# A fused attention and residual-MLP kernel on one core: scores three tiles per visit, second products tile by tile in two PSUM banks, first products with banks of their own

## The chip, the core and the metric

The kernel runs on one core of a Trainium2 chip. The metric is the device time of one execution in microseconds (us), lower is better. Engines are named as the profile names them: PE is TensorE (matmul), PEld its weight load, DVE is VectorE, ACT is ScalarE, POOL is GpSimd and SP is SyncE, whose queue here only starts DMAs.

## The reference

Two layers follow each other. The first is attention with 16 query heads on 4 key/value heads, the second a residual MLP with one product over tokens and two over channels:

```python
batch, n_q_heads, n_kv_heads, seq, head_dim = (8, 16, 4, 384, 64)
attn = softmax(q @ k.T / sqrt(64)); x = attn @ v      # per head; heads side by side give x: 8 x 384 x 1024
a1 = alpha1 * x + beta1
tok = np.einsum('ts,bsd->btd', w_tok, a1)             # 384 x 384
u = x + lam * tok
a2 = alpha2 * u + beta2
ch = np.maximum(a2 @ w_ch1, 0.0) @ w_ch2              # 1024 -> 4096 -> 1024
return u + lam * ch
```

## The kernel before, in words

**Stages.** Batches 0 and 1 are done one at a time (`main`, L526). Batches 2 to 7 are done as three pairs (`pair`, L661). A pair's two channel products are computed by the seven-product scheme that replaces the eight block products of a 2 x 2 block multiplication; the seven products are numbered 1 to 7 and called `o` in the code.

- *First products* (L693 to L738): 8 groups, each of 14 steps of 4 matmuls with 384 columns. Each step adds into one of the PSUM tiles X, Y or Z. ACT and DVE read these tiles, and the result `hid` stays in SBUF.
- *Second products* (L740 to L796): for each product `o` in the order 1, 2, 6, 5, 3, 7, 4, for each half `h` of the 16 contraction blocks `t`, for each of three token tiles `ms`, 8 matmuls with 512 columns into the PSUM tile C (L757). Three C tiles live through the whole stage. Products 2, 5, 3 and 4 add on top of what is already in PSUM, so that sums over products cost no engine. After the last half each C tile is read once (L778 to L785), by ACT for product 1 and by DVE for the others. DVE then scales the result (`scaled`, L675), and POOL adds it to the output by DMA (`store`, L519).

**The side work.** While PE does the second products of pair 0 and pair 1, the attention of the next two batches is slipped in between the C matmuls, as two "sides" (`side`, L230). Each side has 18 score tiles (`scores`, L272: 64-row matmuls, then one ACT exp over 128 x 1024), and for each of 8 head pairs `p`: `av` (L307: 18 small matmuls; then on DVE a reciprocal, a multiply into `xr`, and the two operations that make `a1`), `tok` (L341: 9 matmuls over tokens; then a DVE add and a multiply that makes `a2`), and `flip` (L420: SP spills `xr` to the output and transposes `a2` by DMA). For the last three head pairs of every second side `turn` (L429) does that transposition on PE, with a copy by ACT.

**What sets the order.** The order on each engine is the order in which the program is written (a manual schedule, L802). `pair` is a generator: in the second products it yields after every 4th matmul in effect, which makes 84 slots of 4 C matmuls. A dictionary `plan` says which side work is issued after which slot. For sides of batches 4 to 7 it is the table at L447 to L461: two score tiles every 4 slots (`scores2`), and `av`, `tok`, `flip` of head pair p at slots 4(p+1)+3, +6 and +8. The second of the two sides is shifted by 36 slots (L972). The operand sums for the next pair's first products (`sums_a`, L590, three DVE operations each) stand at slots 75, 75, 76 and 78 (L973), and `sum_w1` (L622) makes weight sums on DVE during product 4 (L746). The second-product weights (28 tiles of 512 KB, `w2s`) are fetched by SP (`fetch`, L636) into the ring `w1` of 6 slots; the last two tiles go to `pad`. The ring also takes the first-product weights (`load_w1`, L183, on POOL's queue).

**PSUM before.** The pairs have three pools that stay open to the end: `sc` (2 buffers of 2 banks: score tiles, `tok`, `turn`, and Y), `acc` (3 banks: X, C and one of the Z) and `one` (1 bank: `av`, and one of the Z).

Of the kernel before, what the change touches and what calls it, by code (L numbers as in the profile page):

```python
# [12 lines left out]
def kernel(  # L13
# [182 lines left out]
    def three():  # L196
        if pairs:
            return pairs["sc"].tile([P, 2, 4, P], f32, tag="sc", name="sc", bufs=2)
        return threes[0].tile([P, 2, 4, P], f32, tag="sc", name="sc", bufs=3)

    def one():
        if pairs:
            return pairs["one"].tile([P, 4, P], f32, tag="one", name="one", bufs=1)
        return three()[:, 0]
# [25 lines left out]
    def side(b):  # L230
# [72 lines left out]
        def scores2(i):  # L303
            for k in range(2):
                scores(2 * i + k)

        def av_piece(p, hh):  # L307
            if hh == 0:
                if first:
                    avs[p] = bank([P, 2, NST, D1], "mm", "av")  # L310
                else:
                    avs[p] = one().rearrange("p k s -> p (k s)")[:, :2 * NST * D1].rearrange(
                        "p (h st d) -> p h st d", h=2, st=NST)
            av = avs[p]
            hk = (2 * p + hh) // G
            for sq in range(NST):
                m = NST * hh + sq
                for sk in range(NST):
                    k = (p * NST + sk) * NST + m // 2
                    nc.tensor.matmul(out=av[:, hh, sq, :], lhsT=ess[k // 4][:, m % 2, k % 4, :],  # L320
                                     rhs=vb[:, sk, hk, :], start=(sk == 0), stop=(sk == NST - 1))
            if hh == 0:
                return
            rinv = sb.tile([P, 2, NST, 1], f32, tag="rinv", name="rinv", bufs=1)
            nc.vector.reciprocal(out=rinv, in_=av[:, :, :, D:])
            if not first:
                xr[p] = sb.tile([P, NST, P], f32, tag="xr", name="xr", bufs=3)
            nc.vector.tensor_tensor(out=x_of(p).rearrange("p st (h d) -> p h st d", h=2), in0=av[:, :, :, :D],  # L328
                                    in1=rinv.to_broadcast([P, 2, NST, D]), op=MUL)
            if first:  # L330
                return
            t = sb.tile([P, NST, P], f32, tag="a1f", name="a1f", bufs=2)
            nc.vector.tensor_tensor(out=t, in0=x_of(p), in1=bc(g1, p), op=MUL)
            a1s[p] = sb.tile([P, NST, P], bf, tag="a1", name="a1", bufs=2)
            nc.vector.tensor_tensor(out=a1s[p], in0=t, in1=bc(h1, p), op=ADD)  # L335
# [100 lines left out]
        if not first:  # L436
# [10 lines left out]
            if (b - NPL) // 2 > 0:  # L447
# [5 lines left out]
                for j in range(9):  # L453
                    put(4 * j, scores2, j)
                for p in range(NP):
                    put(4 * (p + 1) + 3, av, p)
                    put(4 * (p + 1) + 6, tok, p)
                    put(4 * (p + 1) + 8, flip, p)
                    if by_pe(p):
                        put(4 * (p + 1) + 8 + (p == NP - 3), turn, p)  # L460
# [175 lines left out]
    def fetch(i, n, at=None):  # L636
        if at is None:
            w2_slots[i, n] = w1_free.pop(0)
            at = ring[:, w2_slots[i, n]]
        else:  # L640
            w2_slots[i, n] = None
        w2_at[i, n] = at
        nc.sync.dma_start(out=at, in_=w2s[n])

    def free(slot):
        if slot is None:
            return
        w1_free.append(slot)
        if queue:
            f, *a = queue.pop(0)  # L650
            f(*a)

    queue = [m for i in range(NB) for m in [(load_w1, c) for c in order1[2 if i else RING:]]
             + [(fetch, i, n) for n in range(SLOTS - 2 if i + 1 < NB else SLOTS)] + [(load_w1, c) for c in order1[:2] if i + 1 < NB]]
# [5 lines left out]

    def pair(i):  # L661
        b0 = NPL + 2 * i
        acc = pairs["acc"]
# [3 lines left out]
        def begin_end(ms):  # L667
            ends[ms] = t = piece().bitcast(f32)
# [6 lines left out]
        def scaled(o, b, ms, dw, t):  # L675
            if o != 2:
# [11 lines left out]

        def finish(ts):
# [3 lines left out]
        for g in range(NH // 2):  # L693
            X, Y, snap = {}, {}, {}
            for k, (o, e) in enumerate(SEQ1):
                t = 2 * g + e
                lo, hi = bias1[:, t:t + 1], bias1[:, NH + t:NH + t + 1]
                if o == 1:
                    X[e] = acc.tile([P, 512], f32, tag="acc", name="X", bufs=3)
                if o == 7:  # L700
                    Y[e] = pairs["sc"].tile([P, 2, 512], f32, tag="sc", name="Y", bufs=2)[:, 0]
                if o == 2:
                    Z = acc.tile([P, 512], f32, tag="acc", name="Z", bufs=3) if e else pairs["one"].tile(
                        [P, 512], f32, tag="one", name="Z", bufs=1)
# [35 lines left out]
        X = [[(0, 512, acc.tile([P, 512], f32, tag="acc", name="C", bufs=3))] for _ in range(NST)]  # L740
        snap = {}
        where = {2: (0, 0), 3: (0, 1), 7: (1, 1), 4: (1, 0)}
        for k, o in enumerate(PLACE2):
            for h in range(2):
                for ms in range(NST):
                    if o == 4 and not last and 1 < 3 * h + ms < 5:  # L746
                        sum_w1(0, (5, 7, 6)[3 * h + ms - 2])
                    if o == 5 and not last and h and ms < 2:
                        fetch(i, SLOTS - 2 + ms, pad[:, (1 + ms) * 2048:(2 + ms) * 2048])
                    if last and (o, h) in ((6, 1), (7, 0)):  # L750
                        (lift_end if o == 7 else begin_end)(ms)
                    if last and (o, h, ms) == (7, 0, NST - 1):
                        X[ms] = [(c0, c1, pairs["sc"].tile([P, 2, 512], f32, tag="sc", name="C", bufs=2)[:, 0, :c1 - c0])
                                 for c0, c1 in ((0, 384), (384, 512))]
                    for (c0, c1, x), t in ((c, t) for c in X[ms] for t in range(8 * h, 8 * h + 8)):
# [3 lines left out]
                                         start=(o in (1, 6, 7) and t == 0), stop=(t == NH - 1), skip_group_check=True)  # L759
                        if t % 4 == 3 and ms == NST - 1 and c1 == 512:  # L760
# [6 lines left out]
                        if t % 8 == 3 and c1 == 512:  # L767
                            flush(1)
                            yield 1
                    if h == 1 and not (last and o == 4):  # L770
# [6 lines left out]
                        for c0, c1, x in X[ms]:  # L777
                            if o == 1:  # L778
                                nc.scalar.copy(out=snap[o, ms], in_=x)
                            elif o in (6, 5):  # L780
                                tt(out=snap[o, ms], in0=x, in1=snap[1, ms], op=ADD)
                            elif o == 2:
                                tt(out=t, in0=x, in1=lam_t[:, :512], op=MUL)
                            else:
                                tt(out=t[:, c0:c1], in0=x, in1=snap[{3: 1, 7: 5, 4: 6}[o], ms][:, c0:c1], op=ADD)  # L785
                        if o not in (1, 6, 5):
                            later.append((scaled, o, b0 + bb, ms, dw, t))
                    if o in (2, 6) and (h, ms) in ((0, 1), (0, 2), (1, 0), (1, 1)):
                        r = [(0, 1), (0, 2), (1, 0), (1, 1)].index((h, ms))
                        ts = slice(4 * r, 4 * r + 4)  # L790
                        if o == 2:
                            tt(out=hid[:, ts, 0], in0=hid[:, ts, 3], in1=hid[:, ts, 0], op=SUB)
                        else:
                            tt(out=hid[:, ts, 4], in0=hid[:, ts, 4], in1=hid[:, ts, 0], op=SUB)
# [5 lines left out]
    with tc.manual_schedule(engines=order):  # L800
# [162 lines left out]
        for i in range(NB - 1):  # L963
# [6 lines left out]
            for u, f, h in ((10, flip_q, 0), (17, flip_k, 0), (18, flip_q, 2), (25, flip_q, 4), (33, flip_k, 2), (33, flip_q, 6)):  # L970
                put(ps, 1, u, f, c + 1, h, 2)
            put_all(ps, 1, side(c + 1)[1], lambda u: u + 36)  # L972
            for j, u in ((1, 75), (0, 75), (2, 76), (3, 78)):  # L973
                put(ps, 1, u, sums_a, j)
        for ps in range(NPL + NB):
# [8 lines left out]
            if ps == NPL - 1:  # L984
                side_banks.close()
                mm_banks.close()
                for name in ("sc", "acc", "one"):
                    pairs[name] = ST(tc.psum_pool(name=name, bufs=3))
# [3 lines left out]
        assert not plan  # L992
# [28 lines left out]
```

## Time and profile before

| | |
|---|---|
| median of 3 runs | 743.85 us (743.79 to 745.54) |
| the profiled execution's own time | 745.27 us |
| its span, from the first to the last instruction | 743.5 us |
| granted TensorE clock, mean | 0.999 |
| DVE busy, share of the span | 69% |
| ACT busy, share of the span | 43% |
| main(0) and main(1) until PE starts the first products of pair 0 | 244.2 us |
| pair 0: first products, second products with two sides | 72.8 us, 101.9 us |
| pair 1: first products, second products with two sides | 73.0 us, 101.9 us |
| pair 2: first products, second products without sides | 72.9 us, 72.8 us |

The stage times are the starts of the first matmul of each stage on PE in the trace. In a timeline each row gives the start in us from the span's start, the length in us, the engine, the line, the operation with out<-in, and how many instructions the row merges; a bracket at the end gives the idle time of the engine before the row and what ended it. A row of a windows table gives a stretch, its length, and then for PE, PEld, DVE, ACT and POOL the busy time with the number of instructions, the granted clock, the DMA share and GB/s.

### The profile page before, as it was taken

Reading aid. Unit: us, or ns where it says so; the run is one execution under the profiler, and the core shown is the slowest. Engines: PE = TensorE matmul, PEld = TensorE weight load, DVE = VectorE, ACT = ScalarE, POOL = GpSimd, SP = SyncE. Lnnn points to the kernel's source line nnn. Section 1 sums busy time; section 2 is a strip of 40 time slices with the busy share of each in tenths; the row PEclk is TensorE's granted clock in tenths of the full one; section 3 lists DMA queues with packets and bytes.
Section 4 is the critical chain, followed back from the end, with each engine's and each line's share of the span. In section 5 each row is a group of like instructions: output and inputs, shape, how many; then the busy total and the mean of one; then the engine's idle time right before and its main releaser. Section 6 shows DMA issues by size and latency. Waiting matters only on the chain.

```text
span 743.5 us, 14441 instructions
## 1 busy us (share of the span) xinstructions
PE 731.1 (98%) x5708; PEld 416.1 (56%) x5769; DVE 514.6 (69%) x998; ACT 319.3 (43%) x458; POOL 163.4 (22%) x211
## 2 busy tenths in 40 slices
PE   8999999999999999999999999999999999999997
PEld 5866555566555566645555566655555566654444
DVE  7763366567687889748778977747957987762354
ACT  7632431334332566653443366664334166660000
POOL 9434220420000232201003433210002331000011
PEclk9999999999999999999999999999999999999999
DMA  9999999999998999999979999998988998935976
GB/s 185 194 201 200 207 219 168 172 184 204 221 275 243 178 222 214 256 219 213 272 246 205 200 174 174 173 216 181 246 278 221 183 165 115 162 117 176 291 210 158
DMA packets 218017, 151.32 MB, mean 204 GB/s; under 512 B 88660, under 2 KB 197060, under 8 KB 217948
## 3 DMA queue, kind: packets, MB, share of 16 engines
q0 software_dynamic: 120304, 64.60, 65.8%
q1 hardware_dynamic: 97100, 85.39, 42.3%
q8 instruction: 45, 0.74, 0.4%
q10 hardware_dynamic: 544, 0.39, 0.2%
q14 instruction: 24, 0.20, 0.1%
HBM read 154.84 MB, written 38.27 MB: 260 GB/s over the span
## 4 chain that ended last, share of the span: by engine, by line
PE 85%; DMA 8%; POOL 2%; issue 2%; DVE 2%; POOLq 0%; DVEq 0%
PE C L757 29%; PE X L707 17%; PE Y L707 8%; PE ch L575 8%; PE h L537 7%; PE Z L707 4%; PE sc L280 4%; PE sc L345 3%; DMA ops<-a 3%; DMA w<-in_moe_w_ch_dram 2%; PE one L320 2%; DMA q_raw<-in_q_dram 2%; PE sc L320 1%; POOL w L185 1%; DMA rows<-in_moe_lam_dram 1%
## 5 line engine op out<-in xcount | busy, mean ns | idle before, releaser
L757 PE MATMUL C<-w,arena 128*128 128x512 bf16 (+2 forms) x949 | 219.9, 372 | 2.3
L289 ACT ACTIVATE es<-sc 128x1024 bf16<-128x1024 f32 x126 | 121.8, 1022 | 162.7 <-PE sc L280 158.6
L757 PEld LDWEIGHTS <-arena 128*128 128x128 bf16 x1040 | 93.7, 98 | 99.8 <-issue 7.6
L712 ACT ACTIVATE hT<-X,bias 128x384 f32<-128x384 f32 x144 | 83.7, 581 | 67.4 <-PE X L707 60.4
L707 PEld LDWEIGHTS <-w 128*128 128x128 bf16 x768 | 75.1, 98 | 50.3 <-issue 0.4
L185 POOL DMA_DIRECT2D w<-in_moe_w_ch_dram x68 | 62.4, 924 | 128.9 <-PE X L707 68.2
L575 PE MATMUL ch<-arena,hT 128*128 128x512 bf16 x366 | 87.9, 379 | 1.0 <-issue 0.3
L522 POOL DMA_DIRECT2D out_dram<-hT x33 | 29.3, 887 | 261.5 <-DVE hT L677 135.7
L537 PE MATMUL h<-ops,w 128*128 128x384 bf16 (+1 forms) x480 | 83.7, 327 | 1.9 <-DVE hT L548 0.9
L707 PEld LDWEIGHTS <-pad 128*128 128x128 bf16 x576 | 56.4, 98 | 37.2
L707 PE MATMUL X<-ops,w 128*128 128x384 bf16 x384 | 70.5, 326 | 0.0
L707 PE MATMUL X<-ops,pad 128*128 128x384 bf16 x384 | 70.3, 326 | 0.0
L537 PEld LDWEIGHTS <-w 128*128 128x128 bf16 x480 | 45.1, 98 | 32.3 <-issue 2.8
L575 PEld LDWEIGHTS <-hT 128*128 128x128 bf16 x384 | 34.7, 98 | 36.8 <-issue 2.5
L352 DVE TENSOR_TENSOR xr<-sc,xr 128x384 f32<-128x384 f32 x56 | 31.1, 555 | 34.1 <-PE sc L345 34.1
L320 PEld LDWEIGHTS <-es 128*128 128x128 bf16 x1008 | 38.3, 97 | 12.4
L280 PE MATMUL sc<-qT,kT 64*128 64x384 bf16 (+2 forms) x576 | 43.8, 272 | 0.9 <-DVE xr L328 0.2
L345 PEld LDWEIGHTS <-wtokT 128*128 128x128 bf16 x576 | 37.4, 98 | 12.9 <-DVE a L335 2.7
L707 PE MATMUL Z<-ops,w 128*128 128x384 bf16 x192 | 39.1, 326 | 0.0
L707 PE MATMUL Y<-ops,w 128*128 128x384 bf16 x192 | 39.1, 326 | 0.0
L714 DVE TENSOR_TENSOR arena<-Y,hT 128x384 bf16<-128x384 f32 x48 | 26.8, 558 | 17.3 <-ACT hT L712 15.0
L345 PE MATMUL sc<-a,wtokT 128*128 128x128 bf16 x504 | 37.3, 219 | 0.1
(140 smaller groups left out, 858.2 us busy)
## 6 DMA issues: line engine op xcount, KB each, us to landing
w<-w2s SPq DMA_DIRECT2D x80, 512.0 KB, 4.7
w<-in_moe_w_ch_dram POOLq DMA_DIRECT2D x68, 512.0 KB, 9.9
out_dram<-xr SPq DMA_DIRECT2D x56, 192.0 KB, 5.6
out_dram<-hT POOLq DMA_DIRECT2D x33, 256.0 KB, 6.9
arena<-in_moe_w_ch_dram POOLq DMA_DIRECT2D x16, 512.0 KB, 19.8
w2s<-arena SPq DMA_DIRECT2D x28, 256.0 KB, 3.5
q_raw<-in_q_dram POOLq DMA_DIRECT2D x28, 192.0 KB, 10.4
w2s<-pad SPq DMA_DIRECT2D x16, 256.0 KB, 2.7
```

Of the source, the lines that this page charges most:

```text
L185: nc.gpsimd.dma_start(out=w1[:, w1_slots[c]], in_=w1src[:, :, c * CW * P:(c + 1) * CW * P])
L280: nc.tensor.matmul(out=sc[:, hh, k % 4:k % 4 + n], lhsT=kT[r, 2 * p // G, BLK[hh][sk], :], rhs=qT[r, p, st:st + n, :], start=True, stop=True)
L289: nc.scalar.activation(out=e, in_=sc, func=EXP, scale=scale_qk)
L320: nc.tensor.matmul(out=av[:, hh, sq, :], lhsT=ess[k // 4][:, m % 2, k % 4, :], rhs=vb[:, sk, hk, :], start=(sk == 0), stop=(sk == NST - 1))
L345: nc.tensor.matmul(out=ps[:, tt, :], lhsT=wtokT[:, st, tt * P:(tt + 1) * P], rhs=a1s[p][:, st, :], start=(st == 0), stop=(st == NST - 1 an ...
L352: nc.vector.tensor_tensor(out=u, in0=ps, in1=u, op=ADD)
L522: nc.gpsimd.dma_start(out=at, in_=o, accum_op=ADD)
L537: nc.tensor.matmul(out=ps[:, :n], lhsT=w1[:, w1_slots[c], dt, j * P:(j + 1) * P], rhs=a2T[:, dt, :n], start=(dt == 0), stop=(dt == NDT - 1))
L575: nc.tensor.matmul(out=ps, lhsT=hT[:, nt, ms * P:(ms + 1) * P], rhs=w2[:, row(nt)[0], row(nt)[1], cs], start=(i == 0), stop=(i == NNT - 1))
L707: nc.tensor.matmul(out=ps, lhsT=tb[g, o][:, dt, e * P:(e + 1) * P], rhs=opb(LEFT1[o])[:, dt], start=(o in (1, 2, 7) and dt == 0), stop=(dt ...
L712: nc.scalar.activation(out=snap[o, e], in_=ps, func=IDENT, bias=hi if o == 5 else lo)
L757: nc.tensor.matmul(out=x, lhsT=hid[:, t, LEFT2[o], ms * P:(ms + 1) * P], rhs=rhs[:, t % 4 * 512 + c0:t % 4 * 512 + c1], start=(o in (1, 6, ...
```

## The change

- **Score visits.** The table for the sides of batches 4 to 7 has six visits of three score tiles (`scores3`) at slots 0, 6, 12, 21, 26 and 31 in place of nine visits of two. In two of the six visits the third exp is issued after the next `av`. `av`, `tok` and `flip` (now directly behind `tok`) get new slots. The second side is shifted by 39 slots, and `sums_a` moves to slots 78, 78, 80 and 82.
- **Second products tile by tile.** In pairs 0 and 1, for all products but 4, one C tile takes all 16 contraction blocks at once. It starts from zero in one of two banks, so the sums over products that PSUM made before are now made by DVE: product 2 is added to product 1 and scaled later, product 7 is read twice.
- **Banks.** The pools are no longer open to the end. `share_banks` closes the pools of one stage and opens those of the next: X (3 banks), Y (3) and Z (2) for the first products; `sc` (3 buffers of 2 banks, now also for `av`) and `acc` (2 banks) for the second products.
- **Buffers and fetches.** `xr` has four buffers instead of three and `a1f` one instead of two. Two places in `pad` join the ring for the second-product weights, so that eight tiles can be there. Four first-product weight chunks of the next pair are loaded early instead of two. In pair 2, the tiles `ends` lie in the `es` buffers.

The core of the diff:

```diff
     def three():
         if pairs:
-            return pairs["sc"].tile([P, 2, 4, P], f32, tag="sc", name="sc", bufs=2)
+            return pairs["sc"].tile([P, 2, 4, P], f32, tag="sc", name="sc", bufs=3)
...
     def one():
-        if pairs:
-            return pairs["one"].tile([P, 4, P], f32, tag="one", name="one", bufs=1)
         return three()[:, 0]
...
-                xr[p] = sb.tile([P, NST, P], f32, tag="xr", name="xr", bufs=3)
+                xr[p] = sb.tile([P, NST, P], f32, tag="xr", name="xr", bufs=4)
...
-            t = sb.tile([P, NST, P], f32, tag="a1f", name="a1f", bufs=2)
+            t = sb.tile([P, NST, P], f32, tag="a1f", name="a1f", bufs=1)
...
-                for j in range(9):
-                    put(4 * j, scores2, j)
+                for j in range(6):
+                    put((0, 6, 12, 21, 26, 31)[j], scores3, j, j in (2, 5))
                 for p in range(NP):
-                    put(4 * (p + 1) + 3, av, p)
-                    put(4 * (p + 1) + 6, tok, p)
-                    put(4 * (p + 1) + 8, flip, p)
+                    put((4, 10, 14, 18, 24, 29, 33, 35)[p], av, p)
+                    put((8, 15, 17, 22, 27, 34, 36, 38)[p], tok_flip, p)
                     if by_pe(p):
-                        put(4 * (p + 1) + 8 + (p == NP - 3), turn, p)
+                        put((37, 39, 41)[p - NP + 3], turn, p)
...
+    def padded(i, n):
+        return n % 8 > 5 or i + 1 < NB and n >= SLOTS - 2
+
+    def fetch(i, n):
+        w2_slots[i, n] = slot = (pad_free if padded(i, n) else w1_free).pop(0)
+        w2_at[i, n] = ring[:, slot] if slot < RING else pad[:, (slot - RING + 1) * 2048:(slot - RING + 2) * 2048]
+        nc.sync.dma_start(out=w2_at[i, n], in_=w2s[n])
...
+    for i in range(NB):
+        heads = [(load_w1, c) for c in order1[:4]] if i + 1 < NB else []
+        queue += [(load_w1, c) for c in order1[4 if i else RING:]] + [(fetch, i, n) for n in range(SLOTS - 2)] + heads[:2]
+        queue += [(fetch, i, n) for n in (SLOTS - 2, SLOTS - 1)] + heads[2:]
...
+    pair_banks = ExitStack()
+
+    def share_banks(*names):
+        pair_banks.close()
+        for name in names:
+            pairs[name] = pair_banks.enter_context(tc.psum_pool(name=name, bufs=3))
+
     def pair(i):
         b0 = NPL + 2 * i
-        acc = pairs["acc"]
+        share_banks("X", "Y", "Z")
...
         def begin_end(ms):
-            ends[ms] = t = piece().bitcast(f32)
+            ends[ms] = t = sb.tile([P, 512], f32, tag="es", name="ends", bufs=EB)
...
         def scaled(o, b, ms, dw, t):
-            if o != 2:
+            if o != 2 or not last:
...
         finish(slice(NH - 2, NH))
-        X = [[(0, 512, acc.tile([P, 512], f32, tag="acc", name="C", bufs=3))] for _ in range(NST)]
+        share_banks("sc", "acc")
...
         for k, o in enumerate(PLACE2):
-            for h in range(2):
+            whole = not last and o != 4
+            for h in range(1 if whole else 2):
                 for ms in range(NST):
...
+                    if whole:
+                        X[ms] = [(0, 512, acc.tile([P, 512], f32, tag="acc", name="C", bufs=2))]
+                    elif not last and h == 0:
+                        X[ms] = c_banks(ms)
+                    upto = NH if whole else 8 * h + 8
...
-                                tt(out=snap[o, ms], in0=x, in1=snap[1, ms], op=ADD)
-                            elif o == 2:
+                                tt(out=snap[o, ms], in0=x, in1=snap[1 if last or o == 6 else 6, ms], op=ADD)
+                            elif o == 2 and last:
                                 tt(out=t, in0=x, in1=lam_t[:, :512], op=MUL)
                             else:
-                                tt(out=t[:, c0:c1], in0=x, in1=snap[{3: 1, 7: 5, 4: 6}[o], ms][:, c0:c1], op=ADD)
+                                base = {2: 1, 3: 1 if last else 5, 7: 5, 4: 6}[o]
+                                tt(out=t[:, c0:c1], in0=x, in1=snap[base, ms][:, c0:c1], op=ADD)
+                            if o == 7 and not last:
+                                tt(out=snap[6, ms], in0=x, in1=snap[6, ms], op=ADD)
...
-            for u, f, h in ((10, flip_q, 0), (17, flip_k, 0), (18, flip_q, 2), (25, flip_q, 4), (33, flip_k, 2), (33, flip_q, 6)):
+            for u, f, h in ((10, flip_q, 0), (17, flip_k, 0), (18, flip_q, 2), (28, flip_q, 4), (33, flip_k, 2), (33, flip_q, 6)):
                 put(ps, 1, u, f, c + 1, h, 2)
-            put_all(ps, 1, side(c + 1)[1], lambda u: u + 36)
-            for j, u in ((1, 75), (0, 75), (2, 76), (3, 78)):
+            put_all(ps, 1, side(c + 1)[1], lambda u: u + 39)
+            for j, u in ((1, 78), (0, 78), (2, 80), (3, 82)):
                 put(ps, 1, u, sums_a, j)
```

The helper `c_banks(ms)` gives the C tile of product 4: from `acc` for the first two token tiles and from `sc` for the third. `pad_free`, `pump` and the new `free` let a fetch wait in the queue until a ring slot or a place in `pad`, whichever it needs, is free.

## The prediction

> **What bounds the kernel now.** I read the page first, then the stages, then the starts of PE's rows, then DVE where the stages meet. Part 1 of the page:
>
> ```profile
> PE 731.1 (98%) x5708; PEld 416.1 (56%) x5769; DVE 514.6 (69%) x998; ACT 319.3 (43%) x458; POOL 163.4 (22%) x211
> ```
>
> PE is busy for 98% of the span at a granted clock of 0.999. Only fewer PE microseconds can make the kernel faster, and any wait put on PE makes it slower by its full length. The windows table over the second products of pair 0 (with two sides) and of pair 2 (without):
>
> ```profile
> 317.00:418.90 101.90, 100.95 (x905) 53.62 (x921) 74.81 (x147) 38.23 (x43) 13.98 (x16) 1.00 1.03 229
> 666.70:739.50 72.80, 72.42 (x363) 34.66 (x367) 30.55 (x46) 2.11 (x4) 7.68 (x9) 1.00 0.75 218
> ```
>
> The sides cost PE 29.1 us per pair, and there DVE is busy for 74.8 of 101.9 us: PE never waits long for it, but it is not far from full. PE's timeline at the end of that stage:
>
> ```profile
> 402.27 1.02 PE L757 MATMUL C<-w,arena 128*128 128x512 bf16 x4
> 403.23 0.61 PE L280 MATMUL sc<-qT,kT 64*128 64x256 bf16 x8
> 403.77 1.04 PE L757 MATMUL C<-w,arena 128*128 128x512 bf16 x4
> ...
> 410.50 0.67 PE L345 MATMUL sc<-a,wtokT 128*128 128x128 bf16 x9
> ...
> 418.94 1.61 PE L707 MATMUL X<-ops,w 128*128 128x384 bf16 x8
> ```
>
> Elsewhere in the stage eight C matmuls take 1.73 us from start to start (327.28 to 329.01), so a slot of four takes 0.865. Here four take 0.96 because 64-row matmuls follow: 0.10 is lost on entering a score visit. The visit then takes 0.54 for two tiles whose columns, two row halves at a time, need 0.43: about 0.10 is lost on leaving. A visit costs **0.19** beside its tiles. `av` takes 0.53, `tok` 0.50, `turn` 0.17.
>
> DVE's timeline over the same end, from tok of the last head pair (L352) to the third C tile of product 4 (L785):
>
> ```profile
> 411.20 0.56 DVE L352 TENSOR_TENSOR xr<-sc,xr 128x384 f32<-128x384 f32 x1 [0.44 <-PE sc L345]
> 411.79 0.56 DVE L356 TENSOR_TENSOR obuf<-xr,vecs 128x384 bf16<-128x384 f32 x1
> 412.27 0.35 DVE L591 TENSOR_TENSOR ops<-ops 128x384 bf16<-128x384 bf16 x1
> ...
> 414.13 0.69 DVE L631 TENSOR_TENSOR pad<-w 128x1024 bf16<-128x1024 bf16 x1
> ...
> 417.19 0.69 DVE L785 TENSOR_TENSOR hT<-C,hT 128x512 f32<-128x512 f32 x1
> ...
> 418.99 0.69 DVE L785 TENSOR_TENSOR hT<-C,hT 128x512 f32<-128x512 f32 x1
> ...
> 420.32 0.68 DVE L785 TENSOR_TENSOR hT<-C,hT 128x512 f32<-128x512 f32 x1
> ```
>
> DVE works without a gap and reads the last C tile at 421.00, **2.1 us after PE has begun the next stage** at 418.94. Nothing waits for that today: of the first X tiles the second waits 0.15 for its own bank (the row at 418.94 is 1.61 long where others of x8 are 1.46).
>
> **The change, part by part.** The sum is made against the profiled execution: span 743.5, its own time 745.27, while the median of the runs is 743.85. I add the sum to the median.
>
> *Score visits.* Four sides with 6 visits instead of 9: 12 visits fewer, 12 x 0.19 = **-2.3 us**. The matmuls stay the same in number and shape, and the C matmuls are only reordered (216 ns each either way).
>
> *Small waits of before.* Per pair, in the starts of PE's rows: two `tok` 0.10 late, one `turn` 0.15, the X tile 0.15. All stand at places that the change rebuilds; I take them as gone, 2 x 0.5 = **-1.0** (bound: 0).
>
> *Banks: a wait at each stage change.* In the changed kernel's instruction order the first X matmul of a pair waits not for the reader of its own bank but for DVE's read of the last tile of the pools just closed: the third C tile of product 4 for pairs 1 and 2, the last ch tile of main(1) for pair 0. Behind this waiting instruction stands all of PE. The price for pair 0 can be read today:
>
> ```profile
> 244.23 1.46 PE L707 MATMUL X<-ops,w 128*128 128x384 bf16 x8
> 244.43 0.69 DVE L582 TENSOR_TENSOR obuf<-ch,vecs 128x512 f32<-128x512 f32 x1 [1.57 <-PE ch L575]
> ```
>
> DVE ends at 245.12; with 0.06 until PE starts (as after the 0.15 wait above), X starts **0.95** late. That is the bare price with an idle DVE, and the lower bound for the other two. There DVE is behind. I count from the end of slot 72. PE: av(6) 0.53, slot, tok(5) 0.50, slot, av(7) 0.53, slot, tok(6) 0.50, slot, turn 0.17, slot, 0.15 for its buffer, tok(7) 0.50, five slots of 0.865 in all: tok(7) ends at 7.2. Then six slots and two turns, 5.5: the stage ends at 12.7. DVE, in the new order: two reads and a scaling of product 7's last tile until 1.3; av(6) 1.88 (reciprocal 0.19 and three of 0.56; 402.72 to 404.60 today); tok(5) 1.06; av(7) 1.88; tok(6) 1.06; one weight sum 0.60: tok(7)'s add starts at 7.75. From there to the end of the last C read is today 421.00 - 411.20 = 9.80, with three weight sums; the new order has the same operations but one weight sum (0.60) ahead of tok(7): 9.20. The last read ends at 16.95, and PE starts X at 17.0 instead of 12.7: **4.3 us**, twice: +8.6. The lag grew from 2.1 because tok(7) moves from slot 74 to 77 and av(7) from 71 to 74, while 9 us of DVE work stay behind it. After the wait DVE is less behind than today, so nothing else is late in the first products; `sum_w1` and the X, Y, Z reads there have 56.5 of 73.0 us.
>
> *Closer side work.* DVE must make `a1` between av and tok, and read av before the third score tile may take its buffer. First side, counted from the end of slot 33: av(6) is made by 2.6, a `hid` difference 0.88, tok(5) 1.06, a C read 0.60, av(7) 1.88: `a1` of pair 7 is there at 7.1. PE wants tok(7) at 6.4 (five slots 4.33, two av 1.06, two tok 1.0): +0.8 with waking. Counting slots 12 to 26 alike, x of av(4) ends at 17.4 when the third tile of the fifth visit wants it: 0.1 to 0.2 late with the weight load. The second side has no `hid` differences and pays only the 0.15 above, which the 12.7 holds and the 4.3 does not. Two pairs: 2 x (0.8 + 0.2) = **+2.0** and 2 x 0.15 = **+0.3**. The bounds are 0 and, with both places on each side, 4.
>
> *At nothing.* The DVE additions (product 7 read twice, product 2 scaled: 6 x 0.69 per pair) lie in DVE's idle 27 us, and where not they are in the ledgers. ACT's three exps (3 x 1.02) end before the av that wants them, 2 to 4 slots later. `a1f` is written and read by DVE alone. `xr` has four buffers for spills that land in 5.6 us. The SP flips wait for DVE directly behind `tok`, with fetches behind them; a weight tile is wanted 10 or more slots after its fetch and lands in 4.7. The last two go to `pad` at slots 70 and 71 and are wanted at slot 78: 7 slots and seven visits, 9.6 us, against 6.3 for the pad row. The later flip_q is wanted 23 slots on. The end of pair 2 keeps its order.
>
> Sum: -2.3 - 1.0 + 0.95 + 8.6 + 2.0 + 0.3 = **+8.55**: 743.85 + 8.55 = **752.4 us**.
>
> [...]
>
> **Rivals.**
> 1. *The wait does not bind (faster or even).* Place: first X of each pair. If DVE's last read were done when PE arrives, or PE did not wait for it, the result is -3.3 to -1.0: 740.6 to 742.9. It decides from a DVE lag of 0. Against: even an idle DVE needs 0.95 after the last matmul. Chance 0.03.
> 2. *DVE keeps up.* Three boundaries at 0.95, clusters 0 to 2.3: -3.3 + 2.85 + 0 to 2.3: 743.4 to 745.7. It needs DVE to lose 3.3 us of work before the boundary; the rows show it gapless over the last 9.8. Chance 0.05.
> 3. *Also a late transfer.* The two pad tiles (3.3 us of margin), with two weight loads of 9.9 us issued at the same slots. If they land 2 us late in both pairs: 756.4. For it: the DMA share is 1.3 in 402 to 419. Against: the ring has more room than before. Chance 0.10.
>
> The forecast (749 to 755.5) has 0.82. The range leaves out rivals 1 and 2 and the far part of 3: 747.5 to 756. A measurement of this kernel tells about 0.3% (2.2 us): faster 0.03, within it 0.05, slower 0.92.
>
> **What would show it.** Right: an idle stretch of about 4 us on PE before the first X of pairs 1 and 2, ended by DVE's read of a C tile, and 0.95 before pair 0; 24 visits of 64-row matmuls in place of 36; first products still 73 us; second products with sides 1 us shorter before waits. Wrong: X starting directly after C, or PE waits on DMA in the last slots.

## The result, and the profile after

The changed kernel takes 754.28 us (median of 5 runs, 752.46 to 756.75), the kernel before 744.49 us beside it (743.79 to 745.54): a ratio of 1.0129, interval 1.0104 to 1.0155. It is slower by 1.3%; the forecast was 752.4 us. The profiled run is the fastest of the five: 752.46 us, with a span of 750.7 us at a mean clock of 0.997. The engines' line of its page, and then the windows of the first products of pair 0, its second products, the first and second products of pair 1, and the second products of pair 2 (columns: length, then busy time and count of PE, PEld, DVE, ACT and POOL, granted clock, DMA share, GB/s):

```profile
PE 729.8 (97%) x5710; PEld 419.1 (56%) x5769; DVE 521.3 (69%) x1010; ACT 318.7 (42%) x458; POOL 163.4 (22%) x211
```

```profile
243.28:316.09 72.81, 72.81 (x449) 43.85 (x450) 62.43 (x116) 48.49 (x80) 22.36 (x28) 1.00 1.25 210
316.09:421.45 105.36, 99.64 (x905) 54.55 (x921) 80.23 (x157) 38.10 (x43) 15.94 (x19) 1.00 1.01 224
421.45:495.93 74.48, 74.48 (x449) 44.42 (x449) 54.01 (x99) 48.49 (x80) 23.18 (x29) 0.98 1.25 179
495.93:601.30 105.37, 99.80 (x906) 54.57 (x921) 80.25 (x157) 38.10 (x43) 15.01 (x17) 1.00 0.97 215
674.10:747.00 72.90, 72.39 (x362) 34.65 (x367) 30.63 (x46) 2.08 (x4) 7.66 (x9) 1.00 0.75 218
```

PE's busy time in the second products with sides fell from 100.95 to 99.6 to 99.8 us, as fewer visits should make it, and yet each of these stages grew from 101.90 to 105.4 us. So 5.6 to 5.7 us of each is waiting, where it was 0.95. Pair 0's first products and pair 2's second products are as they were. Pair 1's first products are 1.5 us longer, with PE busy throughout but a clock of 0.98. What ended PE's waits, over the whole span (total, times, longest):

```profile
PE X L720 <- DVE hT L818: 5.3, 2, 3.1
PE C L781 <- DMA pad<-w2s: 2.6, 3, 1.8
...
PE sc L339 <- DVE a L329: 1.2, 2, 0.6
PE X L720 <- DVE obuf L575: 0.8, 1, 0.8
```

L818 is DVE's read of a C tile (L785 before), L339 is `tok`, L575 the read of the lead's last ch tile. PE's timeline at the end of pair 0, then DVE's over the same end:

```profile
414.53 1.89 PE L781 MATMUL C<-pad,arena 128*128 128x512 bf16 x8 [1.76 <-DMA pad<-w2s]
...
421.45 1.83 PE L720 MATMUL X<-ops,w 128*128 128x384 bf16 x8 [2.28 <-DVE hT L818]
423.08 1.49 PE L720 MATMUL Y<-ops,w 128*128 128x384 bf16 x4
...
426.38 0.81 PE L720 MATMUL Y<-ops,w 128*128 128x384 bf16 x4
```

```profile
412.12 0.55 DVE L346 TENSOR_TENSOR xr<-sc,xr 128x384 f32<-128x384 f32 x1
...
415.64 0.68 DVE L818 TENSOR_TENSOR hT<-C,hT 128x512 f32<-128x512 f32 x1
...
418.37 0.68 DVE L818 TENSOR_TENSOR hT<-C,hT 128x512 f32<-128x512 f32 x1
...
420.62 0.68 DVE L818 TENSOR_TENSOR hT<-C,hT 128x512 f32<-128x512 f32 x1
```

DVE starts the add of the last `tok` at 412.12 and ends the last C read at 421.30; X starts at 421.45, where the kernel before had let X start 2.1 us ahead of the end of that read. The bracket at 414.53 is a wait the sum did not have: the second of the two pad tiles of product 4 is late (the four matmuls on the first one started at 411.58 without a wait). From the starts of PE's rows the two waits are 1.92 and 2.44 us here, 4.36 together; in pair 1 they are 1.14 and 3.22 us, again 4.36. The row at 423.08 shows a third thing: four matmuls take 1.49 us where four take 0.81 later, half speed: the granted clock is 0.50 from 423.0 to 424.5.

The profiled spans differ by 7.2 us: +3.5 in each of two second products, +1.5 in pair 1's first products, +0.9 in front of pair 0, -0.3 behind the last products, and -1.9 in the lead stages, 1.4 of it in main(1)'s first products (57.7 before, 56.3 after). The attention that runs there uses the buffers of `xr` and `a1f`, whose number the diff changes. In the kernel before, PE waits there for transfers (0.60 us at 133.55 for `ops`, 0.26 us at 152.47 for a weight load); in the changed kernel and in every variant below these two waits are gone. That is 0.86 of the 1.4 us. Which part of the change took them away was not tried.

### The profile page after: what moved, and what is told of

Read it like the earlier page. It is cut to its first block, busy times and chain, and to the rows that moved or that the text cites. A ratio compares the mean times of both kernels' runs of the same rounds, so it can differ in the third digit from the quotient of the medians.

```text
span 750.7 us, 14462 instructions
## 1 busy us (share of the span) xinstructions
PE 729.8 (97%) x5710; PEld 419.1 (56%) x5769; DVE 521.3 (69%) x1010; ACT 318.7 (42%) x458; POOL 163.4 (22%) x211
## 4 chain that ended last, share of the span: by engine, by line
PE 86%; DVE 9%; DMA 2%; issue 2%; ACT 0%; DVEq 0%
PE C L781 23%; PE X L720 17%; PE h L530 10%; PE ch L568 10%; PE Y L720 8%; PE sc L278 4%; PE Z L720 4%; PE sc L314 3%; PE sc L339 3%; DMA pad<-w2s 1%; DMA ops<-a 1%; DVE xr L322 1%; DVE a1f L327 1%; DVE xr L346 1%; DVE hT L818 1%
## 5 line engine op out<-in xcount | busy, mean ns | idle before, releaser
L781 PE MATMUL C<-w,arena 128*128 128x512 bf16 (+2 forms) x731 | 169.3, 372 | 1.7
L781 PE MATMUL C<-pad,arena 128*128 128x512 bf16 (+2 forms) x268 | 63.2, 373 | 2.8 <-DMA pad<-w2s 2.6
L339 PEld LDWEIGHTS <-wtokT 128*128 128x128 bf16 x576 | 37.5, 98 | 13.9 <-DVE a L329 3.0
L278 PE MATMUL sc<-qT,kT 64*128 64x384 bf16 (+2 forms) x576 | 41.5, 271 | 1.6 <-ACT hT L287 0.3
L319 DVE RECIPROCAL rinv<-sc 128x6 f32<-128x6 f32 x56 | 10.7, 191 | 42.8 <-PE sc L314 42.7
L314 PE MATMUL sc<-v,es 128*128 128x65 bf16 x1008 | 39.9, 193 | 0.0
```

Source lines behind the costliest of these rows:

```text
L278: nc.tensor.matmul(out=sc[:, hh, k % 4:k % 4 + n], lhsT=kT[r, 2 * p // G, BLK[hh][sk], :], rhs=qT[r, p, st:st + n, :], start=True, stop=True)
L339: nc.tensor.matmul(out=ps[:, tt, :], lhsT=wtokT[:, st, tt * P:(tt + 1) * P], rhs=a1s[p][:, st, :], start=(st == 0), stop=(st == NST - 1 an ...
L781: nc.tensor.matmul(out=x, lhsT=hid[:, t, LEFT2[o], ms * P:(ms + 1) * P], rhs=rhs[:, t % 4 * 512 + c0:t % 4 * 512 + c1], start=((not last o ...
```

## The experiments

The theory: at each boundary X waits for DVE's read of the last C tile because the pools are closed and opened, and DVE is late because its work behind the last `tok` did not shrink when `tok` moved. The rivals: DVE is late for the operands as well, whatever the banks; or the late transfer sets the end. The ratios are against the kernel before, run beside each:

| run | median us (range) | ratio [interval] |
|---|---|---|
| changed kernel | 754.28 (752.46-756.75) | 1.0129 [1.0104, 1.0155] |
| e1_one_pool | 872.83 (872.68-874.17) | 1.173 [1.1713, 1.1747] |
| e2_no_sums | 749.16 (744.98-751.39) | 1.0057 [1.0036, 1.0078] |
| e3_gate | 755.09 (752.46-757.64) | 1.0156 [1.0133, 1.0178] |
| e4_pool_gate | 873.43 (872.79-875.07) | 1.1737 [1.1719, 1.1756] |
| e5_one_pool_apart | 750.0 (748.81-752.94) | 1.0085 [1.0065, 1.0105] |
| e6_no_boundary | 757.29 (752.86-758.86) | 1.0166 [1.0139, 1.0193] |
| e7_tok_later | 755.07 (753.21-759.24) | 1.0139 [1.0118, 1.016] |
| e9_split_visits | 758.08 (754.72-762.83) | 1.0192 [1.0157, 1.0227] |
| e10_defer | 749.68 (747.89-751.6) | 1.0071 [1.0057, 1.0085] |
| e11_all_waits | 746.92 (746.43-747.36) | 1.0035 [1.0023, 1.0047] |
| e13_all_but_tok | 748.61 (747.96-753.06) | 1.0075 [1.0053, 1.0098] |
| e14_best | 742.17 (741.65-742.8) | 0.997 [0.9958, 0.9982] |

### e1 and e4: one pair of pools, and a trap of my own

```diff
-                if o == 1:
-                    X[e] = pairs["X"].tile([P, 512], f32, tag="X", name="X", bufs=3)
...
+                if o in (1, 7) and e == 0:
+                    two = pairs["sc"].tile([P, 2, 512], f32, tag="sc", name="X" if o == 1 else "Y", bufs=3)
+                    (X if o == 1 else Y).update({0: two[:, 0], 1: two[:, 1]})
```

> The changed kernel with one pair of PSUM pools open over all pairs instead of closing and opening pools between the stages; the order of the work is the same. Theory (the first X matmul waits for DVE's read of the last C tile only because the pools are closed): the waits of 0.95, 2.4 and 3.2 us at the three boundaries go. DVE is as late as before, but the first that needs it is the first Y matmul, 2.9 us later, which reads an operand sum; it is at most 0.7 us late. The waits for the pad tiles of product 4 (1.9 and about 1.1 us) stay and are now on the path by themselves. The half-clock stretch behind the first pair (1.6 us) goes too. Sum: 754.3 - 0.95 - 2.4 - 3.2 - 1.6 = 746 us (745 to 748). Rival 1 (the boundary is a DVE wait whatever the banks, because the operands are late too): the wait moves to the first Y matmul with 2 to 3 us each, 751 to 753. Rival 2 (the transfer is the cause): nothing changes, 754.

> One pair of pools open over all pairs, and the last two weight loads held back: both edits at once. Theory: without the pool wait and without the late transfer, only DVE's late operand sums are left: the first Y matmul waits 0.5 to 1.5 us at two boundaries. From 754.3: - 0.95 - 2 x 4.36 + 2 x 0.8 - 1.6 (half clock) = 744.6 us (743 to 746). Rival (the lag simply moves to the next thing that needs DVE): 2 to 3 us at the first Y matmul, 748 to 750.

Both took 873 us. Neither theory had that. PE's waits in e1:

```profile
PE X L717 <- ACT hT L722: 52.2, 74, 0.7
PE Y L717 <- DVE arena L730: 25.5, 24, 1.7
PE X L717 <- ACT arena L728: 16.1, 24, 0.7
```

The boundary wait for a C read is gone from the list, but X now waits for ACT 74 times. Two X tiles lay in the two halves of one PSUM tile, and a product into one half waited for the ACT copy out of the other, 74 times and 52.2 us in all in e1; with a tile for each, in e5, no such wait is in the list. The runs say nothing reliable on the boundaries; e5 is the mended form.

### e2: less DVE work ahead of the last read

```diff
-            for j, u in ((1, 78), (0, 78), (2, 80), (3, 82)):
-                put(ps, 1, u, sums_a, j)
```

> The changed kernel without the operand sums (sums_a) that DVE makes in the last slots of pairs 0 and 1: it leaves out 12 tensor_tensor operations of 128x384 bf16 per pair, about 3.7 us of DVE work ahead of the last C read; the first products of pairs 1 and 2 then work on unsummed operands. Theory (the boundary wait is DVE's lag behind PE): DVE reads the last C tile about 3.7 us earlier, so it is no longer what ends last; the first X matmul waits for the bare price of about 0.95 us, the pad tile's wait of 1 to 2 us stays ahead of it. 4.36 us per boundary becomes 2 to 3 us, less 1.6 for the half clock: 754.3 - 2 x 1.9 - 1.6 = 749 us (748 to 751). Rival (the lag is set by something else, such as the transfer): the wait at X does not move, 754.

It took 749.16 us. PE's row at the first boundary between pairs, and the wait for the pad tile at the second:

```profile
419.22 0.97 PE L720 MATMUL X<-ops,w 128*128 128x384 bf16 x5 [0.87 <-DVE hT L818]
```

```profile
590.69 1.41 PE L781 MATMUL C<-pad,arena 128*128 128x512 bf16 x4 [3.02 <-DMA pad<-w2s]
```

With 3.7 us less DVE work ahead of it, the wait for the C read is the bare price at both boundaries (0.87 and 0.88 us). So its size in the changed kernel was DVE's backlog. What is left varies with the pad tiles: no wait in pair 0 of this run, 3.02 us in pair 1. The nine runs spread from 745.0 to 751.4 us.

### e3: the weight loads held back

```diff
-        ... + heads[:2]
-        queue += [(fetch, i, n) for n in (SLOTS - 2, SLOTS - 1)] + heads[2:]
+        queue += [(fetch, i, n) for n in (SLOTS - 2, SLOTS - 1)] + [(gate,)] * bool(heads) + heads[2:]
...
+                    if o == 4 and not last and 3 * h + ms == 2:
+                        gate()
```

> The changed kernel with the last two weight loads of a pair held back until the third slot of product 4 (slot 76), so that the two pad tiles are fetched alone. Theory (DVE sets the end, the late transfer is hidden under it): the pad tiles arrive in time, PE's wait for them (1.9 and about 1.1 us) goes, and the wait at the first X matmul grows by as much, to 4.3 us: 754 us, no change (753 to 755.5). Rival (the transfer costs its own time): 754.3 - 3 = 751 us. A second rival (the transfers are late for another cause): the wait for the pad tiles stays at 1 to 2 us.

No change in the time, as expected. The two rows at the end of pair 0:

```profile
413.42 1.89 PE L795 MATMUL C<-pad,arena 128*128 128x512 bf16 x8 [0.63 <-DMA pad<-w2s]
421.48 0.81 PE L732 MATMUL X<-ops,w 128*128 128x384 bf16 x4 [3.41 <-DVE hT L832]
```

The transfer's wait fell by 1.1 us and the wait for DVE grew by as much; X starts where it started (421.48 and 421.45). In pair 1 the transfer's wait did not fall: 0.47 and 0.69 us, against 0.20 and 0.62 in the changed kernel. The fetches were not quite alone either: the two loads start 4.7 us later (406.83 instead of 402.14), while the pad tiles are still on their way. So the loads beside the fetches are at most a part of the lateness, seen in one of the two pairs.

### e5: one pair of pools, each accumulator in a tile of its own

```diff
-        share_banks("X", "Y", "Z")
...
-        share_banks("sc", "acc")
...
+                if o == 1 or (o, e) == (7, 1):
+                    (X if o == 1 else Y)[e] = pairs["sc"].tile([P, 2, 512], f32, tag="sc", name="XY"[o > 1], bufs=3)[:, 0]
+                if (o, e) in ((7, 0), (2, 0)):
+                    Z = pairs["acc"].tile([P, 512], f32, tag="acc", name="YZ"[o == 2], bufs=2)
...
```

> As e1, one pair of pools over all pairs, but each X and Y accumulates in a PSUM tile of its own (two X in the halves of one tile made every product wait for the ACT copy of the other half in e1). Theory: in e1 the boundary waits did go, and all of its 118 us came from the shared tiles; so now the first products are back at 73 us, the waits of 2.4 and 3.2 us at the first X of pairs 1 and 2 are gone, and the waits for the pad tiles (1 to 3 us per boundary, differing from run to run) stand on the path. 754.3 - 5.7 - 1.6 (half clock) = 747 us (745 to 750). The 0.95 us before pair 0 stays, since the pools of the lead are still closed there. Rival (the lag moves to the first product that needs a late DVE result): 750 to 752. Rival on e1 (its loss came from the single buffers, not from the shared tiles): over 800 again.

It took 750.0 us; the middle was missed by 3, the range held. The wait for the C read is gone from the list, and what stood behind it is in the open:

```profile
PE C L778 <- DMA pad<-w2s: 4.9, 2, 3.5
PE Z L718 <- DVE arena L727: 1.5, 3, 0.7
```

The first X of pair 1 on PE, and DVE's read of pair 0's last C tile:

```profile
421.33 1.46 PE L718 MATMUL X<-ops,w 128*128 128x384 bf16 x8
423.25 0.68 DVE L815 TENSOR_TENSOR hT<-C,hT 128x512 f32<-128x512 f32 x1
```

X starts directly behind the last C matmul at both boundaries, here 2.6 us ahead of the end of a read that is as late as ever. So closing the pools made the wait. In the profiled run the pad tiles cost 1.5 and 3.5 us, and the single Z tile 0.4 to 0.7 us three times in pair 0; half speed follows the second pad wait (a clock of 0.51 from 593.55 to 599.20). That run is the slowest of the four (752.94 us), so how much of this makes the 3 us between the middle and the median is not shown. Here X had a tile of its own and started 2.6 us before the last read of another tile ended; with the closed pools it had started 0.15 us after that read (421.45 against 421.30).

### e6 and e7: no closing at all, earlier fetches, a later tok

```diff
-        return n % 8 > 5 or i + 1 < NB and n >= SLOTS - 2
+        return n % 8 > 5 and (i + 1 == NB or n < 22) or i + 1 < NB and n >= SLOTS - 2
...
-                side_banks.close()
-                mm_banks.close()
+                pairs.update(sc=threes[0], acc=mms)
```

e7 adds:

```diff
-                    put((8, 15, 17, 22, 27, 34, 36, 38)[p], tok_flip, p)
+                    put((8, 15, 17, 22, 27, 34, 36, 38 if b % 2 else 40)[p], tok_flip, p)
```

> As e5, and in addition the pools of the lead stages are kept for the pairs as well (nothing is closed before the end), and the two pad tiles of product 4 are fetched some 20 slots earlier, into pad slots that no later tile of product 7 uses; tiles 22 and 23 go to the ring instead. Theory: all three boundary waits and the pad waits are gone: 754.3 - 0.95 - 8.7 - 1.6 (half clock) = 743.0 us (742 to 744.5). Rival (DVE's lag of 2 to 4 us comes back in the first products): 745 to 749.

> As e6, and tok of the last head pair of the first side is issued two slots later (slot 40, behind the next side's first visit), when its a1 is there. Theory: its wait of 0.77 us per pair goes: e6 - 1.5 = 741.5 us (740.5 to 743), which is before's time less the 12 visits. Rival (the tile then waits for an exp instead): as e6.

They took 757.3 and 755.1 us: both expectations failed. PE's waits in e6:

```profile
PE C L772 <- DMA w<-w2s: 5.1, 3, 2.9
PE Y L712 <- DVE ops L585: 3.2, 2, 1.8
```

All three boundary waits at X and the waits for the pad tiles are gone, but two new ones stand in their place. Tiles 22 and 23, which I had sent to the ring, are now fetched only when product 3's tiles free it, and come 0.9 to 2.9 us late. And DVE's lag appears at the first Y, which reads an operand sum: 1.78 and 1.45 us. That is the rival of e5 and e6, at less than its price. In e7 `tok`'s wait for `a1` is gone as well, but the time is not told apart from e6's (753.2 to 759.2 against 752.9 to 758.9). Its profile has new waits, of a `turn` for DVE (0.88 and 2.62 us); e9, with the same move, has none of them, so the move alone does not make them. e13 settles what the move is worth.

### e9: the price of a visit

```diff
-                for j in range(6):
-                    put((0, 6, 12, 21, 26, 31)[j], scores3, j, j in (2, 5))
+                for j in range(6):
+                    for k in range(3):
+                        put((0, 6, 12, 21, 26, 31)[j] + k // 2, scores, 3 * j + k, j in (2, 5) and k == 2)
```

> As e7, but every visit of three score tiles is split into one of two and, one slot later, one of one: the same matmuls in 24 visits more. Theory (a visit costs 0.19 us beside its tiles): e7 + 24 x 0.19 = e7 + 4.6 us, 746 us, with PE's busy time in each second stage 2.3 us up. Rival (the cost lies in the tiles and not in the visit): e7 + 0.

The medians differ by 3.0 us, with scatters wider than that. The second products of pair 0, at a clock of 1.00 in both, tell it better: e7, then e9.

```profile
318.06:421.86 103.80, 100.57 (x923) 54.59 (x922) 75.25 (x145) 38.36 (x43) 13.12 (x15) 1.00 0.95 219
```

```profile
317.41:422.22 104.81, 102.95 (x923) 52.87 (x922) 76.69 (x147) 38.34 (x43) 13.12 (x15) 1.00 0.95 218
```

The same 923 matmul records keep PE busy 2.38 us longer for 12 more visits: 0.198 us each, against 0.19 in the sum. The stage itself is only 1.0 us longer, because PE is idle there for 1.86 us instead of 3.23. In pair 1 both runs have stretches at half speed (a clock of 0.63 from 602.39 to 607.00 in e7, 0.60 from 577.68 to 582.00 in e9), so its busy times can't be compared.

### e10: DVE's work moved behind the last read

```diff
-                    if o == 4 and not last and 1 < 3 * h + ms < 5:
-                        sum_w1(0, (5, 7, 6)[3 * h + ms - 2])
+                    if o == 4 and not last and 1 < 3 * h + ms < 4:
+                        sum_w1(0, (5, 7)[3 * h + ms - 2])
...
-                            if t % 8 == 3:
+                            if t % 8 == 3 and (last or o != 4 or later[:1] and later[0][1] == 7):
                                 flush(1)
...
+        if not last:
+            sum_w1(0, 6)
         flush()
```

> The changed kernel with three DVE operations per boundary moved from ahead of the last C read to behind it: the scalings of the first two C tiles of product 4 and one weight sum, 0.6 us each from start to start; nothing else is moved and nothing left out. Theory (the boundary is DVE's lag, one for one): DVE's last read comes 1.8 us earlier. In the profiled run of the changed kernel each boundary cost 4.36 us of PE waits (pad tile and first X together); now the second costs 2.55, and the first 1.9 (pad tile) + 0.95 (bare) = 2.9. 754.3 - 1.5 - 1.8 = 751 us, 749.5 with the half-clock stretch gone. Rival (the work put behind the boundary is missed there, since the first products read its results): the first products are longer by as much, 754.

It took 749.68 us. Its waits:

```profile
PE C L781 <- DMA pad<-w2s: 4.8, 2, 3.0
PE X L720 <- DVE hT L818: 1.8, 2, 0.9
```

The wait for the C read is the bare 0.88 us at both boundaries, with every result still made; only the pad tiles are above it (1.75 and 3.01 us). The first products did not lose what was put into them (72.8 us in pairs 1 and 2). Between the medians, three operations of 0.6 us in another order made 4.6 us of the 9.8. The two profiled runs differ by 1.6 us only (752.46 and 750.86): the pad wait in pair 1 is longer here (3.01 us), and half speed follows it (a clock of 0.65 from 591.73 to 596.00). What the other 3 us are, no profile shows.

### e11, e13 and e14: all the cures together

e11 keeps the pools as e6 does, defers as e10, and moves `tok` as e7; the second Z of a group goes into the first X's tile, and the pad slots of product 7 hold other tiles:

```diff
-        return n % 8 > 5 or i + 1 < NB and n >= SLOTS - 2
+        return n in ((6, 7, 14, 15, 20, 21, SLOTS - 2, SLOTS - 1) if i + 1 < NB else (6, 7, 14, 15, 22, 23))
...
-                ps = (X[e] if o in (1, 6, 5, 3) else Y[e] if o in (7, 4) else Z)[:, :S]
+                ps = (X[e] if o in (1, 6, 5, 3) else Y[e] if o in (7, 4) else X[0] if e else Z)[:, :S]
```

> All the cures at once: one pair of pools from the lead stages to the end (as e6); the second Z of a group accumulates in the tile of the first X, whose last product is done by then (e5 and e6 lost 0.4 to 0.7 us to a single Z tile three times in pair 0); the work deferred as in e10; tok of the last head pair of the first side two slots later (as e7); and the pad slots of product 7 hold its first two tiles instead of its last two, so that the two pad tiles of product 4 are fetched 2 slots earlier and ahead of the weight loads. Theory: no PE wait above 0.5 us is left in the pairs: before's 744.05 - 2.3 (12 visits) - 0.5 = 741.3 us (740.5 to 743). Rival (transfers are late wherever the ring is full, as in e6 and e7): PE waits for DMA of 1 to 3 us in each pair, with a half-clock stretch behind them, 745 to 750.

> As e11 with tok of the last head pair of the first side back in its place (slot 38). Theory: it waits 0.77 us for its a1, once per pair: e11 + 1.5 = 742.8 us. Rival (the move costs elsewhere what it saves, as it may have in e7): e11 or less.

e11 took 746.92 us instead of 741.3: no wait for a transfer and none for a C read was left, but my own two edits cost 1.6 us (the deferred weight sum, wanted 0.82 us earlier by the second X product in two pairs) and 0.18 us at each of 24 second Z, seen in the starts of PE's rows (4.3 us). e13 differs from it by `tok` alone: 1.7 us in the medians (1.5 expected), and in pair 0's second products 101.02 against 100.25 us, 0.77. e14 mends the two:

```diff
-    SEQ1 = (..., (3, 0), (3, 1), (2, 1), (4, 0), (4, 1))
+    SEQ1 = (..., (3, 0), (3, 1), (4, 0), (2, 1), (4, 1))
...
+                        if o == 4 and ms == NST - 1:
+                            sum_w1(0, 6)
                         for c0, c1, x in X[ms]:
```

> As e11, with its two own losses mended: the second Z of a group goes back to the one Z tile, but its product is issued one place later (behind the first of product 4), so that it neither waits for DVE's read of the first Z nor, as in e11, 0.18 us for the ACT copy of an X, 24 times (4.3 us); and the weight sum that e11 deferred behind the last C read, for which the second X product then waited 0.82 us in two pairs (1.6 us), is made just ahead of that read. Theory: the PE waits are the last thing between the changed order and its saved visits: 746.9 - 4.3 - 1.6 = 741.0 us (740.3 to 742), 3 us under before's 744.1. Rival (the Z product now finds DVE busy elsewhere, or the last C read comes late for a Y): 743 to 746.

It took 742.17 us, 0.2 above the range, and is the only one below the kernel before: 0.997 [0.9958, 0.9982]. Its two second products with sides:

```profile
316.17:416.42 100.25, 98.97 (x906) 54.73 (x922) 76.14 (x148) 38.61 (x43) 13.73 (x16) 1.00 1.03 231
490.23:590.48 100.25, 98.97 (x906) 54.72 (x922) 76.16 (x148) 38.62 (x43) 13.25 (x15) 1.00 0.98 222
```

100.25 against 101.90 before: 1.65 us less in each, 3.3 in both. That is what the change's own idea is worth once little waits. Of it e14 gives back 0.9 us in each of the first products of pairs 1 and 2 (73.8 against 72.9 to 73.0), in waits of 0.2 and 0.4 us.

## Why the prediction was right, step by step

- **Visits, -2.3 and small waits, -1.0.** Right: 0.198 us per visit (e9), and -3.3 for the two terms together in e14. The e14 figure does not part the two.
- **In front of pair 0, +0.95.** Right: 0.8 us of idle in the list of waits, the stage 0.9 us longer.
- **The two boundaries, +8.6.** Right in size, 4.36 each where 4.3 was forecast, and in cause. Only the place was partly another: 1.92 and 1.14 us of the 4.36 were spent one stop earlier, at the pad tiles, and X itself waited 2.44 and 3.22 us instead of 4. DVE's stretch from `tok`'s add to the end of the last read was worked out at 9.20 us and measured at 9.18. e5 shows that the closed pools make the wait, e2 and e10 that DVE's backlog gives it its length.
- **Closer side work, +2.0 and +0.3.** `tok` waits 0.77 us (0.8 forecast) in each pair; the third score tile, put at 0.2, showed no wait. The profile parts no 0.15 us at the second side from the rest. So it was about 1.5.
- **At nothing: the pad tiles.** Here a step failed: "7 slots and seven visits, 9.6 us, against 6.3 for the pad row". In pair 0 the first tile was issued at 402.09 and was there when PE wanted it 9.5 us later. The second was issued at 403.82, was wanted at 412.61, 8.8 us later, and came only at about 414.5, after 10.7 us. The pad tiles made PE wait 1.9 and 1.1 us, and PE waiting on DMA in the last slots was one of the prediction's own signs of being wrong. It cost the sum nothing, because the wait for DVE ended later anyway: e3 turned the one into the other. For the same reason rival 3 was priced wrongly: it came true, if not by 2 us in both pairs, and added nothing to the sum. The two waits run side by side and only the later end counts.
- **Missing from the sum: the clock.** After the first long wait PE ran at half speed for some 3 us (a clock of 0.65 over 4.85 us), 1.5 us of the profiled run. The sum of what the trace shows is -3.3 + 0.95 + 8.7 + 1.5 + 1.5 = 9.4 us; with the -1.9 us in the lead stages and -0.3 at the end, which the prediction did not have either, it is 7.2, the difference of the two spans. The medians differ by 9.8 us. The profiled run is the fastest of the five, so 2.6 us of the 9.8 stand in no profile.
- **What was luck.** The boundaries, most of the sum, were worked out and came out. That the pad tiles' wait lay inside the wait for DVE, and that the missing half speed (+1.5) was nearly balanced by the lead stages (-1.9), was not foreseen: that the forecast of 752.4 us lies 1.9 us under the median is in part luck.
- **Rival 1 and 2** (no wait, or an idle DVE) are what e14 and e2 had to build by hand.

What stays open: why the pad tiles take some 10 us and more, up to 13 (in e5's pair 1, from the issue at 580.43 to 593.55). Holding back two weight loads took 1.1 us off the lateness in pair 0 and nothing in pair 1 (e3), and fetching 2 slots earlier in another slot order removed the waits (e11, e14); what filled the queues in between was not tried by itself.

## What to carry to other kernels

Before one set of buffers is closed for another on a full engine, look for the last reader of anything in the closed set: here the new first writer waited for that reader, not for its own bank's (2.28 and 3.06 us in the changed kernel, no such wait in e5), and the wait went with the reader's backlog (down to 0.87 and 0.88 us in e2, with 3.7 us less of it). A wait can hide others that end before it (in e3 the one for the transfer fell by 1.1 us and the one for DVE grew by as much), so a cure must be measured again after each layer: here the transfer, then the operand sums, then single buffers came up one after the other. Small moves mattered as much as the visits: by the medians, three short operations put behind the last read made 4.6 us (e10; 1.6 between the profiled runs), and a product moved by one place together with a weight sum put back made 4.75 us (e11 to e14), against 2.3 us for the twelve visits saved.

## What the runs showed of the hardware that was not expected

**Half speed after waits of 1.6 to 3.5 us.** The windows of the 4 to 5 us behind a wait, in the changed kernel (2.28 us for DVE at pair 1's first X, preceded by 1.76 us for a transfer) and, in the same kernel, behind 3.06 us at pair 2's first X:

```profile
421.45:426.30 4.85, 4.85 (x20) 2.52 (x21) 3.26 (x5) 1.57 (x3) 1.63 (x2) 0.65 1.44 198
```

```profile
601.30:606.00 4.70, 4.70 (x29) 2.83 (x30) 3.25 (x5) 2.32 (x4) 0.84 (x1) 1.00 1.42 198
```

The granted clock is 0.65 in the one and 1.00 in the other. Of the eleven waits of 2.28 us and more in the pairs of these profiles, eight were followed by a clock of 0.51 to 0.65 over the next 4.3 to 5.7 us (2.28, 2.49, 2.62, 2.94, 3.01, 3.02, 3.41 and 3.46 us) and three by 1.00 (2.34, 2.72 and 3.06 us). A shorter one did it once: behind 1.57 us in e7, with 0.85 us just ahead of it, four matmuls took 1.86 us, where four behind the 0.85 took 1.02. Single waits of 1.75 us (e10) and 1.76 us (the changed kernel) were followed by 1.00. So length alone does not decide it here; what else does, no run shows. The loss in the first row is (1 - 0.65) x 4.85 = 1.7 us, so that the 2.28 us of waiting ahead of it cost 4.0 by this estimate. The kernels with waits of 2.28 us and more in their profiles also scatter more between their runs, over 3.7 to 8.1 us, against 0.9 and 1.15 us for e11 and e14, whose clocks are 0.999 and 1.0 in every run. e13 has no such wait in its profile and spreads over 5.1 us, its two longest runs at clocks of 0.998 and 0.997. How much of the scatter is the waits themselves and how much the clock was not measured.

**A visit's price.** Going from 128-row to 64-row matmuls and back cost 0.198 us of PE's busy time, measured by splitting visits of three tiles into two and one (e9); the rows of the kernel before gave 0.19 for visits of two.
